# A fixed order of 1254 steps replaced by another fixed order

## The chip, the cores and the metric

The kernel runs on one core of one Trainium2 chip. The metric is the device time of one execution in microseconds (us). The engines are PE (TensorE; PEld is its weight load), DVE (VectorE), ACT (ScalarE), POOL (GpSimd) and SP (SyncE, which here only starts transfers).

## What is computed

Linear attention over 8 batches of 8 heads feeds a gated MLP (gMLP). All data are fp32.

```python
q_s = softmax(q, axis=-1);  k_s = softmax(k, axis=2)      # q, k, v: (8, 8, 576, 64)
kv  = einsum('bhsd,bhde->bhde', k_s, v)                   # k_s^T v for each head
x   = einsum('bhsd,bhde->bhse', q_s, kv)                  # heads side by side: (8, 576, 512)
h   = gelu_tanh(x @ w_in);  u, v = h[..., :512], h[..., 512:]
v_n = (v - mean(v)) / sqrt(var(v) + 1e-6) * g_ln
v_s = einsum('ts,bsd->btd', w_sg, v_n) + b_sg[None, :, None]
out = x + (u * v_s) @ w_out
```

(The first einsum sums over the 576 positions s.)

## The kernel before, in words

Every large product is made of three PE products of high and low fp32r parts (high by high, high by low, low by high), so each operand is first split: ACT writes the rounded high part, DVE or POOL subtracts to get the low part. In the names of tiles `_h` is the high part and `_l` the low one, and `vnh`, `vnl`, `gh`, `ulow` are such parts too.

The work is cut into 1254 steps, each a small function called with a batch number and indices, and the text `PLAN` (from line 39) lists all of them in one fixed order. The loop at line 920 reads it and calls one function after the other. Each of DVE, ACT, POOL and SP runs its instructions strictly in the order in which the steps issue them (class `InOrder`), and PE keeps program order too. So the order in `PLAN` decides what stands behind what on each engine. An engine whose next instruction waits makes everything behind it wait. A letter at the end of a step names the engine where there is a choice (V is DVE, G is POOL, A is ACT).

The steps that the text speaks of:

- Weights arrive as 64-bit words in eight pieces f for `w_in` (`load_w_in f`) and four for `w_out`. ACT scales a piece (`wi_a f`), DVE repairs the bits in three instructions (`wi_b`, `wi_c`, `wi_d`), ACT writes the high part (`wi_h`), and `wi_l` the low part. The tile in work is `ot_i`. Pieces 4 to 7 are needed by `hv_mm`, 0 to 3 by `hu_part` and `hu_mm`.
- For each batch b and half of the heads h: `k_sub` and `k_exp` make the exponent of k (tile `kk`), `kv_mm` multiplies it by v, `kv_inv` and `kv_scale` (DVE, tile `kvt`) divide. `q_sub`, `q_exp`, `q_sum` (tile `qd`), `q_swapd` (ACT, tile `qe`), `q_inv` and `q_mul` make the softmax of q (tile `qq`), and `q_turn` transposes it into `qt`. `x_mm` (batch 1) or `xm_mm` (batches 2 to 7) multiply kv by q.
- `hv_mm b i` and `hv_gelu` make v (through two PSUM banks, `ps1`, that are used in turn, also by `kv_mm`). `hv_sq`, `hv_stat`, `hv_pow` (POOL), `hv_norm`, `hv_high` and `hv_low` normalise it and split it into `vnh` and `vnl`.
- `sg_mm`, `hu_mm` and `out_mm` use three double banks (`ps2`) in turn. A bank comes free when `gate`, `hu_gelu` or `out_add` has read it.
- `gate b d` (DVE) is u times v_s, `gate_high` and `gate_low` split it, `out_mm b e` multiplies it by `w_out`, `out_base` adds the two parts of x, `out_add` adds the product, and `out_store` writes the result.

ACT must load a table (ACT_TABLE_LOAD) whenever it goes from exponentials to gelu or back. The compiler puts it right before the first instruction that needs it.

Of the kernel before, what the change touches and what calls it, by code (L numbers as in the profile page):

```python
# [63 lines left out]
hv_pow 0 2, k_mb 2 1, k_mc 2 1, hv_high 0 2, hv_stat 0 4 A, hv_pow 0 4, tail_high 1, k_mb 2 0, k_mc 2 0, load_w_sg 4, ws_h 4, tail_high 0, hv_low 0 2
k_fold 2 1, wo_h 2, hv_mm 1 2, hv_gelu 1 2, k_rota 2 1, ws_l 4 V, k_maxa 2 1, hv_mm 1 1, k_rotb 2 1, ws_l 2 G, tail_again 0, hv_sq 1 3, tail_low 0
ws_l 3 G, sg_mm 0 0, sg_mm 0 2, k_fold 2 0, hv_sq 1 0, k_maxb 2 1, q_max 2 1, q_swapm 2 1, hv_stat 1 0 A, k_rota 2 0, k_sub 2 1 G, q_max 2 0
tail_low 1, k_maxa 2 0, hv_gelu 1 1 A, load_v 2 1, q_top 2 1, q_sub 2 1 G, gate 0 0, k_rotb 2 0, hv_sq 1 1, q_swapm 2 0, k_exp 2 1, q_exp 2 1
sg_mm 0 1, gate_high 0 0, gate 0 2, hv_stat 1 1 A, wo_l 2 G, sg_mm 0 3, wo_l 1 V, hu_mm 1 0, gate_low 0 0 G, gate 0 1, hv_norm 1 0, hv_pow 1 0
k_maxb 2 0, k_sub 2 0 V, q_top 2 0, k_exp 2 0, gate 0 3, gate_high 0 3, gate_high 0 1, q_sub 2 0 V, gate_low 0 1 V, hv_stat 1 3 A, wo_h 3, wo_l 3 G
gate_high 0 2, hv_stat 1 2, load_v 2 0, gate_low 0 2 G, q_exp 2 0, q_sum 2 0, q_swapd 2 0, q_sum 2 1, out_base 0 2 V, wo_l 0 V, gate_low 0 3 G  # L70
kv_mm 2 1, hv_high 1 0, hv_low 1 0, out_base 0 3 V, hv_pow 1 2, kv_mm 2 0, load_k 3 1, k_ma 3 1, out_mm 0 3, q_inv 2 0, q_mul 2 0 1 G, hv_pow 1 1
kv_inv 2 0, load_k 3 0, out_mm 0 1, out_add 0 3, q_swapd 2 1, q_inv 2 1, hu_gelu 1 0, out_mm 0 0, q_mul 2 1 1 V, q_turn 2 1, q_mul 2 0 0 V, q_turn 2 0
out_mm 0 2, out_base 0 1 V, out_base 0 0 G, out_add 0 1, q_mul 2 1 0 G, hv_pow 1 3, hu_mm 1 3, kv_inv 2 1, out_add 0 0, kv_scale 2 1, hu_gelu 1 3
hv_norm 1 2, load_q 3 0, q_turn 2 3, out_add 0 2, out_store 0 2, kv_scale 2 0, hv_norm 1 3, q_max 3 0, hv_norm 1 1, hv_high 1 3, hu_mm 1 2
hv_high 1 1, out_base 1 2 G, q_turn 2 2, hv_low 1 1, k_mb 3 1, k_mc 3 1, hv_low 1 3, hv_high 1 2, k_fold 3 1, k_ma 3 0, hv_low 1 2, hu_gelu 1 2
q_swapm 3 0, q_top 3 0, xm_mm 2, tail_again 1, xm_high 2 0, sg_mm 1 0, xm_high 2 1, xt_high 2, load_q 3 1, xt_low 2, xm_low 2 0, hu_mm 1 1, q_max 3 1
q_swapm 3 1, xm_low 2 1, q_sub 3 0 V, gate 1 0, q_top 3 1, out_store 0 3, k_mb 3 0, k_mc 3 0, out_store 0 1, sg_mm 1 2, k_rota 3 1, k_maxa 3 1
q_sub 3 1 V, load_v 3 0, k_fold 3 0, hu_gelu 1 1, q_exp 3 0, k_rota 3 0, k_maxa 3 0, k_rotb 3 0, q_exp 3 1, hv_mm 2 1, hv_mm 2 3, k_maxb 3 0
q_sum 3 1, gate_high 1 0, sg_mm 1 1, q_sum 3 0, hv_gelu 2 1 A, k_rotb 3 1, k_sub 3 0 G, out_base 1 3 V, hv_gelu 2 3, k_maxb 3 1, k_sub 3 1 G, gate 1 2
gate_low 1 0 V, sg_mm 1 3, hv_sq 2 1, gate 1 1, load_v 3 1, out_base 1 1 G, q_swapd 3 1, q_inv 3 1, q_mul 3 1 0 V, q_turn 3 2, hv_stat 2 1 A  # L80
k_exp 3 0, kv_mm 3 0, kv_inv 3 0, k_exp 3 1, kv_scale 3 0, q_swapd 3 0, gate_high 1 2, gate 1 3, q_inv 3 0, gate_high 1 1, q_mul 3 0 1 V
out_store 0 0, kv_mm 3 1, kv_inv 3 1, kv_scale 3 1, out_base 1 0 G, gate_low 1 1 G, gate_low 1 2 G, hv_pow 2 1, q_mul 3 1 1 V, q_turn 3 3
gate_high 1 3, q_mul 3 0 0 G, hv_mm 2 0, hv_gelu 2 0 A, q_turn 3 1, q_turn 3 0, hv_sq 2 0, hv_stat 2 3, gate_low 1 3 G, out_mm 1 2, load_q 4 1
# [892 lines left out]
```

## Time before, and how to read the profile

| | |
|---|---|
| median of 3 runs | 500.97 us (500.81 to 501.94) |
| profiled execution | 500.59 us, of which the span from first to last instruction is 498.5 us |
| PE busy | 481.5 us, 97% of the span |
| DVE busy | 359.7 us, 72% |
| ACT busy | 282.6 us, 57%, with 32 table loads (41.1 us) |
| POOL busy | 159.8 us, 32% |
| granted PE clock | full level (2.4 GHz) in all 40 slices |

The rows further down come from one profiled execution. A timeline row has its start in us, its duration in us, the engine, the line of the kernel (a helper issues nearly everything, so the line is always the same), the operation, out<-in by tile, and in brackets how long the engine sat idle before it and what ended that. A row with x40 merges 40 instructions. Busy PE includes matmuls that are slowed, and their ends are modelled, so distances between starts are the better measure there.

### The profile page before, as it was taken

To read this page: it belongs to the slowest core of one execution; us is meant where nothing else is said; L and a number is where in the kernel's file an instruction comes from. 1 tells how busy PE (TensorE), PEld (TensorE's weight loads), DVE (VectorE), ACT (ScalarE), POOL (GpSimd) and SP (SyncE) were. 2 spreads that over 40 slices of the span, in tenths; PEclk is the share of its full clock that TensorE was granted. 3 is DMA by queue.
4 is the path that set the end of the run, shared out by engine and by line. 5 is a ranking of instruction groups with operands and counts; after the bars stand their busy time and mean duration, and the time that the engine had idled before them with its cause. 6 is when DMAs were issued, how large, how long until landed. Compare 5 with 4: busy or idle time off the path is not lost.

```text
span 498.5 us, 9491 instructions
## 1 busy us (share of the span) xinstructions
PE 481.5 (97%) x3847; PEld 444.6 (89%) x3847; DVE 359.7 (72%) x618; ACT 282.6 (57%) x605; POOL 159.8 (32%) x126
## 2 busy tenths in 40 slices
...
GB/s 308 384 380 169 171 121 2 94 63 236 4 1 262 106 26 1 7 219 0 168 2 101 174 47 16 104 1 130 217 2 0 46 51 1 1 0 49 49 1 95
DMA packets 16302, 47.51 MB, mean 95 GB/s; under 512 B 1922, under 2 KB 3332, under 8 KB 16260
## 3 DMA queue, kind: packets, MB, share of 16 engines
...
## 4 chain that ended last, share of the span: by engine, by line
PE 52%; DVE 18%; ACT 11%; POOL 2%; issue 2%; ACTq 0%; POOLq 0%; DVEq 0%
PE ps L253 52%; DVE qq L164 3%; DVE qd L164 3%; DVE km L164 2%; POOL kk L164 2%; DVE o L164 2%; ACT L164 2%; DVE qm L164 1%; ACT v L164 1%; DVE qt L164 1%; DVE kf L164 1%; ACT kk L164 1%; ACT ka L164 1%; ACT gh L164 1%; ACT qq L164 1%
## 5 line engine op out<-in xcount | busy, mean ns | idle before, releaser
L164 POOL TENSOR_TENSOR rs<-ve,half 128x1 f32<-128x1 f32 x36 | 29.3, 821 | 131.3 <-DVE ve L164 118.1
L253 PE MATMUL ps<-ulow,wo_h 128*128 128x288 f32 x256 | 55.6, 296 | 0.8 <-POOL ulow L164 0.8
L253 PE MATMUL ps<-gh,wo_h 128*128 128x288 f32 x256 | 55.9, 297 | 0.0
L253 PE MATMUL ps<-ws_h,vnl 128*128 128x288 f32 x256 | 55.0, 296 | 0.5 <-DVE vnl L164 0.5
L253 PE MATMUL ps<-ws_h,vnh 128*128 128x288 f32 x256 | 55.3, 297 | 0.2 <-DVE u L164 0.2
L253 PE MATMUL ps<-gh,wo_l 128*128 128x288 f32 x256 | 55.4, 295 | 0.0
L253 PE MATMUL ps<-ws_l,vnh 128*128 128x288 f32 x256 | 54.9, 296 | 0.0
L164 DVE TENSOR_TENSOR u<-ps,u 128x576 f32<-128x576 f32 x32 | 23.5, 746 | 42.5 <-PE ps L253 37.6
L164 ACT ACTIVATE u<-ps 128x576 f32<-128x576 f32 (+2 forms) x36 | 21.2, 595 | 42.7 <-PE ps L253 42.5
L164 ACT ACT_TABLE_LOAD x32 | 41.1, 1283 | 2.9 <-PE ps L253 1.2
L164 ACT CAST gh<-u 128x576 fp32r<-128x576 f32 x32 | 20.8, 668 | 38.4 <-DVE u L164 38.3
L253 PEld LDWEIGHTS ps<-ulow,wo_h 128*128 128x128 f32 x256 | 41.3, 188 | 1.1 <-POOL ulow L164 1.1
L253 PEld LDWEIGHTS ps<-ws_h,vnh 128*128 128x128 f32 x256 | 41.3, 188 | 1.0 <-DVE u L164 0.4
L253 PE MATMUL ps<-x_h,wi_h 128*128 128x288 f32 (+2 forms) x256 | 40.6, 298 | 1.4 <-DVE o L164 0.8
L253 PEld LDWEIGHTS ps<-gh,wo_h 128*128 128x128 f32 x256 | 41.4, 188 | 0.6
L253 PEld LDWEIGHTS ps<-ws_h,vnl 128*128 128x128 f32 x256 | 41.1, 188 | 0.7 <-DVE vnl L164 0.7
L253 PEld LDWEIGHTS ps<-gh,wo_l 128*128 128x128 f32 x256 | 41.4, 188 | 0.0
L253 PEld LDWEIGHTS ps<-ws_l,vnh 128*128 128x128 f32 x256 | 41.0, 188 | 0.0
L164 DVE TENSOR_TENSOR o<-ps,o 128x576 f32<-128x576 f32 (+1 forms) x33 | 23.9, 732 | 23.2 <-PE ps L253 22.5
L253 PE MATMUL ps<-x_h,wi_l 128*128 128x288 f32 (+2 forms) x256 | 39.9, 296 | 0.0
L253 PE MATMUL ps<-x_l,wi_h 128*128 128x288 f32 (+2 forms) x256 | 39.8, 295 | 0.0
L253 PE MATMUL ps<-wi_h,x_h 128*128 128x512 f32 x144 | 39.5, 396 | 0.3 <-ACT wi_h L164 0.2
(128 smaller groups left out, 1089.8 us busy)
## 6 DMA issues: line engine op xcount, KB each, us to landing
...
```

The source lines that it names most:

```text
L164: ins = op(*args, **kw)
L253: tc.keep_in_program_order(nc.tensor.matmul(*args, **kw))
```

## The change

The text `PLAN` is replaced. The 1254 steps are the same, but 67 of them change between V and G, and nearly all stand elsewhere. By kind, the steps that DVE gives to POOL on balance are 5 `gate_low`, 4 `q_mul`, 2 `q_sub` and 2 `wo_l`. POOL gives to DVE 2 `k_sub`, 3 `out_base` and 1 `ws_l`. DVE has 7 instructions fewer, POOL 7 more. ACT has 34 table loads for 32. Nothing else is edited. A few lines of the text, cut:

```diff
 PLAN = """
...
-k_top 1 0, q_swapm 1 0, k_top 1 1, wi_a 6, hu_part 0 3 0, hu_gpart 0 3 0, wi_l 7 V, q_exp 1 1, kb_mm 1 0, wi_b 6, wi_c 5, kb_mm 1 1, wi_c 6, q_top 1 0
-load_w_out 2, q_swapd 1 0, hv_mm 0 0, kv_scale 1 0, q_inv 1 0, q_mul 1 0 0 V, load_w_out 1, b_l G, q_mul 1 0 1 G, hv_gelu 0 0 A, ws_h 1, q_turn 1 0
-q_mul 5 0 0 V, k_maxa 5 1, hv_gelu 4 3, hv_stat 4 0 A, sg_mm 3 2, hu_gelu 3 2, hv_gelu 4 1 A, k_rotb 5 1, k_exp 5 0, k_maxb 5 1, q_turn 5 0
-out_store 2 1, k_sub 5 1 G, k_exp 5 1, gate_high 3 1, hv_stat 4 3, q_swapd 5 1, q_inv 5 1, gate 3 3, load_v 5 0, hv_mm 4 2, hv_gelu 4 2
-out_base 3 1 G, kv_mm 5 0, gate 3 2, gate_high 3 2, q_turn 5 1, gate_low 3 1 V, q_mul 5 1 0 G, gate_low 3 2 V, hv_sq 4 1, hv_pow 4 3, gate_high 3 3
...
+wi_a 6, wi_a 5, wi_d 4, hu_gpart 0 0 0, k_top 1 0, wi_h 4, load_w_sg 2, k_top 1 1, q_max 1 0, wi_h 7, hu_part 0 1 0, hu_gpart 0 1 0, load_w_out 3
+q_sum 1 0, wi_l 4 G, wi_h 5, wi_l 5 G, kv_mm 1 0, kv_inv 1 0, b_l G, k_exp 1 1, q_swapd 1 0, q_sum 1 1, kv_scale 1 0, hu_gpart 0 2 1, load_w_sg 3
+q_swapd 1 1, hv_mm 0 0, hv_gelu 0 0 A, q_inv 1 0, wo_a 3, q_mul 1 0 0 V, q_turn 1 0, q_inv 1 1, wo_a 0, q_mul 1 1 0 V, load_g, hu_gpart 0 3 1
+q_turn 5 1, k_exp 5 1, hv_norm 4 0, gate_low 3 1 G, gate 3 2, hv_norm 4 2, gate_high 3 2, hu_mm 3 3, q_turn 5 3, hv_high 4 3, gate_low 3 2 V
+k_exp 5 0, kv_mm 5 1, kv_inv 5 1, hu_gelu 3 3, kv_mm 5 0, gate 3 3, gate_high 3 3, gate_low 3 3 G, load_q 6 1, kv_inv 5 0, load_q 6 0, load_v 6 1
...
```

Three places show what the new text does to the order on an engine. In each pair the first fence is the kernel before.

DVE, batch 1, where pieces 4 to 7 of `w_in` are repaired (`ot_i_6` is piece 6, `ot_i_5` piece 5, `kt1` and `qm1` are maxima of k and q, `kk1_0` is k of half 0):

```order
L164 TENSOR_REDUCE qm1_0_445<-qq1_0_373 128x36
L164 TENSOR_REDUCE kt1_0_449<-ps1_0_80 128x2
L164 TENSOR_REDUCE kt1_1_456<-ps1_1_81 128x2
L164 TENSOR_TENSOR wi_l_62<-ot_i_7_317,wi_h_61 128x4x128
L164 TENSOR_SCALAR ot_i_6_458<-ot_i_6_458 128x512
L164 SCALAR_TENSOR_TENSOR ot_i_5_405<-raw_i_wo_h_91,ot_i_5_405 128x512
L164 SCALAR_TENSOR_TENSOR ot_i_6_458<-raw_i_wo_l_92,ot_i_6_458 128x512
L164 TENSOR_TENSOR qm1_0_445<-qm1_0_445,qs1_0_451 128x36
L164 SCALAR_TENSOR_TENSOR ot_i_6_458<-raw_i_wo_l_92,ot_i_6_458 128x512
```

The same place on DVE now:

```order
L163 TENSOR_REDUCE kt1_0_442<-ps1_0_80 128x2
L163 TENSOR_REDUCE kt1_1_447<-ps1_1_81 128x2
L163 TENSOR_REDUCE qm1_0_449<-qq1_0_354 128x36
L163 TENSOR_SCALAR ot_i_6_436<-ot_i_6_436 128x512
L163 TENSOR_TENSOR wi_l_62<-ot_i_7_331,wi_h_61 128x4x128
L163 SCALAR_TENSOR_TENSOR ot_i_6_436<-raw_i_wo_l_92,ot_i_6_436 128x512
L163 TENSOR_SCALAR ot_i_5_438<-ot_i_5_438 128x512
L163 SCALAR_TENSOR_TENSOR ot_i_6_436<-raw_i_wo_l_92,ot_i_6_436 128x512
L163 TENSOR_TENSOR qm1_0_449<-qm1_0_449,qs1_0_468 128x36
```

Piece 6 is now begun before `wi_l` of piece 7 and ends before piece 5. On ACT its `wi_a 6` has moved ahead of `wi_h 4`, `wi_h 7`, some gelus and the `q_swapm 1 0` copies, all of which stood before it. `load_w_in 6` has moved one place up on SP's queue, past `load_q 1 0`.

ACT, batches 0 and 1, at the first table load for gelu behind the exponentials of batch 1 (`qe1_0` and `qe1_1` are `q_swapd 1 0` and `1 1`, `u0_2` is gelu of u, `v0_0` is `hv_gelu 0 0`, `ws_h` and `ot_o` are weights):

```order
L164 ACTIVATE kk1_1_368<-kk1_1_368 128x1280
L164 COPY qe1_0_571<-qd1_0_563 32x36 x4
L164 ACT_TABLE_LOAD
L164 ACTIVATE v0_0_598,sm0_0_599<-ps1_0_80 128x512
L164 CAST ws_h_63<-ghws_1_492 128x576
L164 COPY qe1_1_604<-qd1_1_568 32x36 x4
L164 ACTIVATE u0_1_439<-ps2_2_79 128x320
L164 ACTIVATE u0_2_447<-ps2_0_77 128x320
```

The same place on ACT now:

```order
L163 ACTIVATE kk1_1_340<-kk1_1_340 128x1280
L163 COPY qe1_0_575<-qd1_0_544 32x36 x4
L163 ACT_TABLE_LOAD
L163 ACTIVATE u0_2_414<-ps2_2_79 128x320
L163 COPY qe1_1_587<-qd1_1_580 32x36 x4
L163 ACTIVATE v0_0_604,sm0_0_605<-ps1_0_80 128x512
L163 ACTIVATE ot_o_3_609<-raw_o_vnl_365 128x512
L163 ACTIVATE ot_o_0_616<-raw_o_vnh_372 128x512
```

The table load now stands before a gelu of `u0_2`, whose product `hu_part 0 2 1` is made before `kv_mm 1 0`, and `q_swapd 1 1` stands before `hv_gelu 0 0`.

DVE, outputs of batch 0 (`o0_e<-ps2...,o0_e` is `out_add 0 e`, `o0_e<-x_h0,x_l0` is `out_base 0 e`, `kr2` and `kvt2` are `kv_inv` and `kv_scale` of batch 2, `v1` is `hv_norm`, `qt2` is `q_turn`):

```order
L164 TENSOR_TENSOR o0_1_1345<-x_h0_308,x_l0_310 128x576
L164 TENSOR_TENSOR o0_1_1345<-ps2_0_77,o0_1_1345 128x576
L164 TENSOR_SCALAR kr2_1_1377<-ps1_0_80 128x2
L164 RECIPROCAL kr2_1_1377<-kr2_1_1377 128x2
L164 TENSOR_TENSOR o0_0_1347<-ps2_1_78,o0_0_1347 128x576
L164 TENSOR_TENSOR kvt2_1_1381<-ps1_0_80,kr2_1_1377 128x128
L164 SCALAR_TENSOR_TENSOR v1_2_895<-v1_2_895,mv1_2_1150,g_bc_67 128x512
L164 STREAM_TRANSPOSE qt2_1_1388<-qq2_1_725 128x576
L164 TENSOR_TENSOR o0_2_1169<-ps2_2_79,o0_2_1169 128x576
```

The same place on DVE now:

```order
L163 TENSOR_TENSOR o0_3_1215<-ps2_2_79,o0_3_1215 128x576
L163 TENSOR_TENSOR o0_0_1326<-x_h0_303,x_l0_308 128x576
L163 SCALAR_TENSOR_TENSOR v1_2_995<-v1_2_995,mv1_2_1138,g_bc_67 128x512
L163 TENSOR_SCALAR kr2_1_1332<-ps1_1_81 128x2
L163 RECIPROCAL kr2_1_1332<-kr2_1_1332 128x2
L163 TENSOR_TENSOR kvt2_1_1335<-ps1_1_81,kr2_1_1332 128x128
L163 TENSOR_TENSOR o0_1_1246<-ps2_1_78,o0_1_1246 128x576
L163 TENSOR_TENSOR o0_2_1253<-ps2_0_77,o0_2_1253 128x576
```

The bank `ps2_0_77`, which `hu_mm 1 3` takes next on PE in both kernels, is read by `out_add 0 1` before and by `out_add 0 2` now, directly behind `out_add 0 1`.

On PE, `kv_mm 5 0` and `5 1` stood right behind `hv_mm 4 2`. Now `sg_mm 3 3` and `hu_mm 3 3` stand between `hv_mm 4 1` and them.

## Rows read from the trace of the kernel before

**Rows 1.** The page, first line: span of the profiled execution.

```profile
span 498.5 us, 9491 instructions
```

**Rows 2.** Stretches: us, busy us (instructions) by engine, PE clock, DMA share, GB/s.

```profile
4.00:34.00 30.00, 26.35 (x252) 21.91 (x253) 29.55 (x62) 26.10 (x51) 12.41 (x10) 1.00 1.02 386
34.00:52.00 18.00, 16.04 (x160) 13.29 (x161) 14.59 (x24) 16.55 (x33) 11.94 (x9) 1.00 0.52 180
52.00:98.00 46.00, 45.66 (x350) 40.10 (x342) 43.56 (x79) 39.03 (x101) 25.83 (x19) 1.00 0.29 96
98.00:155.00 57.00, 54.75 (x469) 49.38 (x468) 53.03 (x88) 32.63 (x71) 25.09 (x18) 1.00 0.27 89
...
270.00:495.00 225.00, 225.00 (x1736) 214.12 (x1734) 136.10 (x230) 98.73 (x203) 45.56 (x37) 1.00 0.16 58
```

**Rows 3.** Waits of PE, 98 to 155 us: total us, times, longest us.

```profile
PE ps L253 <- POOL ulow L164: 0.8, 1, 0.8
PE ps L253 <- DVE o L164: 0.8, 1, 0.8
PE ps L253 <- DVE vnl L164: 0.5, 1, 0.5
```

**Rows 4.** Timeline of DVE near 34 us: start, us, instruction, [idle before <-releaser].

```profile
33.65 0.70 DVE L164 TENSOR_TENSOR wi_l<-ot_i,wi_h 128x512 fp32r<-128x512 f32 x1
35.62 0.43 DVE L164 TENSOR_SCALAR ot_i<-ot_i 128x512 uint32<-128x512 uint32 x1 [1.27 <-ACT ot_i L164]
```

**Rows 5.** Timeline of ACT near 35 us.

```profile
34.92 0.67 ACT L164 ACTIVATE ot_i<-raw_i_wo_l 128x512 f32<-128x512 f32 x1
```

**Rows 6.** Timeline of ACT, 45 to 49 us.

```profile
45.53 1.28 ACT L164 ACT_TABLE_LOAD   x1 [1.17 <-PE ps L253]
46.83 0.60 ACT L164 ACTIVATE v<-ps 128x512 f32<-128x512 f32 x1
...
48.23 0.91 ACT L164 COPY qe<-qd 32x36 f32<-32x36 f32 x4
```

**Rows 7.** Timeline of DVE near 49 us.

```profile
49.17 0.20 DVE L164 SCALAR_TENSOR_TENSOR qd<-qd,qe 128x36 f32<-128x36 f32 x1 [1.93 <-ACT qe L164]
```

**Rows 8.** Timeline of PE, 40 to 57 us.

```profile
40.74 1.39 PE L253 MATMUL ps<-vv,kk 128*64 128x65 f32 x40 [0.71 <-ACT kk L164]
...
49.65 0.70 PE L253 MATMUL ps<-qt,kvt 64*64 64x288 f32 x2
51.32 1.20 PE L253 MATMUL ps<-qt,kvt 64*64 64x288 f32 x14 [0.97 <-DVE qt L164]
52.44 1.19 PE L253 MATMUL ps<-wi_h,x_h 128*128 128x512 f32 x4
...
55.42 1.20 PE L253 MATMUL ps<-qt,kvt 64*64 64x288 f32 x16
56.55 0.53 PE L253 MATMUL ps<-x_h,minus 128*128 128x288 f32 x2
```

**Rows 9.** Timeline of PE near 268 us.

```profile
268.29 0.92 PE L253 MATMUL ps<-vv,kk 128*64 128x65 f32 x24 [1.29 <-ACT v L164]
```

**Rows 10.** DVE groups, 98 to 155 us: count | busy us, mean ns | idle before.

```profile
L164 DVE TENSOR_TENSOR qq<-qq,qd 128x576 f32<-128x576 f32 x5 | 7.8, 1562 | 0.1
...
L164 DVE TENSOR_TENSOR ulow<-u,gh 128x576 fp32r<-128x576 f32 x1 | 3.1, 3079 | 0.0
```

**Rows 11.** Tile qd on DVE, whole span: duration ns min/median/max.

```profile
L164 DVE TENSOR_TENSOR qq<-qq,qd x17: 695/758/2033, 13.3 to 381.8; 128x576 f32<-128x576 f32 x16, 128x512 f32<-128x512 f32 x1
L164 DVE SCALAR_TENSOR_TENSOR qd<-qd,qe x14: 155/198/2947, 44.8 to 362.3; 128x36 f32<-128x36 f32 x14
```

**Rows 12.** POOL groups, whole span: count | busy us, mean ns | idle before.

```profile
L164 POOL TENSOR_TENSOR kk<-kk,km 128x1280 f32<-128x1280 f32 x9 | 27.0, 3004 | 38.1 <-issue 15.9 <-DVE km L164 12.4 <-PE ps L253 9.7
L164 POOL TENSOR_TENSOR ulow<-u,gh 128x576 fp32r<-128x576 f32 x16 | 24.8, 1550 | 30.7 <-ACT gh L164 16.2 <-DVE ulow L164 14.3
...
L164 POOL TENSOR_TENSOR qq<-qq,qd 128x576 f32<-128x576 f32 (+2 forms) x15 | 19.5, 1298 | 34.3 <-DVE qd L164 27.8 <-ACT u L164 2.8 <-ACT kb L164 2.4
```

More of the change, by code (lines that the diff above doesn't have):

```diff
@@ L64 @@
[L64 to L83, printed above, removed]
@@ L100 @@
-hv_gelu 4 0 A, q_swapm 5 1, q_top 5 1, hu_mm 3 3, k_maxa 5 0, out_add 2 3, out_store 2 3, hv_low 3 3, hv_low 3 2, k_mb 5 1, q_sub 5 1 G, q_exp 5 1
-hv_pow 3 0, hv_high 3 0, out_store 2 0, hv_low 3 0, hv_sq 4 0, hv_mm 4 1, hu_gelu 3 3, hu_mm 3 1, hu_gelu 3 1, q_swapm 5 0, q_top 5 0, k_mc 5 1
-k_fold 5 1, q_sub 5 0 V, q_sum 5 1, sg_mm 3 0, sg_mm 3 1, out_base 3 3 G, k_rotb 5 0, q_exp 5 0, q_sum 5 0, k_maxb 5 0, hv_mm 4 3, k_sub 5 0 G
-out_base 3 0 V, load_v 5 1, q_swapd 5 0, q_inv 5 0, gate 3 0, gate 3 1, hu_mm 3 2, gate_high 3 0, gate_low 3 0 G, sg_mm 3 3, k_rota 5 1, q_mul 5 0 1 G
@@ new lines @@
+k_maxa 3 1, k_maxb 3 0, sg_mm 1 0, q_swapm 3 0, q_top 3 0, hu_mm 1 1, hu_gelu 1 1, k_sub 3 0 V, gate 1 0, k_rotb 3 1, k_maxb 3 1, out_store 0 0
+hv_mm 2 3, q_sub 3 0 G, q_exp 3 0, sg_mm 1 1, sg_mm 1 3, q_sum 3 0, gate 1 1, k_exp 3 0, q_swapd 3 0, gate_high 1 1, gate_high 1 0, out_base 1 0 V
+k_sub 3 1 G, k_exp 3 1, sg_mm 1 2, q_inv 3 0, hv_mm 2 1, q_top 3 1, q_sub 3 1 V, gate_low 1 0 G, q_exp 3 1, q_sum 3 1, hv_gelu 2 3, gate 1 2, gate 1 3
+q_mul 3 0 0 G, q_mul 3 0 1 G, q_swapd 3 1, q_inv 3 1, hv_gelu 2 1 A, gate_high 1 2, kv_mm 3 1, kv_inv 3 1, hv_sq 2 1, gate_low 1 1 G, kv_scale 3 1
@@ new lines @@
+q_swapm 4 1, q_inv 4 0, k_mb 4 0, k_mc 4 0, q_top 4 1, hu_mm 2 2, q_sub 4 1 G, q_mul 4 0 0 G, q_exp 4 1, hv_pow 2 4, tail_high 2, q_sum 4 1
+k_fold 4 0, hv_low 2 2, tail_again 2, hu_gelu 2 2, q_turn 4 0, hv_norm 3 2, hv_mm 3 3, hu_mm 2 1, tail_high 3, tail_low 3, hv_sq 3 1, hu_mm 2 0
+k_rota 4 0, out_base 2 3 G, hu_gelu 2 1, q_swapd 4 1, hv_gelu 3 0 A, tail_low 2, sg_mm 2 1, hu_gelu 2 0, sg_mm 2 0, q_mul 4 0 1 G, sg_mm 2 3
+q_inv 4 1, k_maxa 4 0, hv_pow 3 2, k_rotb 4 0, k_maxb 4 0, q_turn 4 1, gate 2 1, gate_high 2 1, gate 2 0, hv_gelu 3 3 A, gate_high 2 0, load_q 5 0
@@ new lines @@
+sg_mm 3 1, q_inv 5 0, hv_gelu 4 3, out_add 2 3, k_fold 5 0, q_sub 5 1 V, q_exp 5 1, q_sum 5 1, hu_mm 3 1, hu_gelu 3 1, gate 3 1, hv_stat 4 3
+hv_norm 4 3, q_swapd 5 1, k_rota 5 0, k_maxa 5 0, q_mul 5 0 0 G, sg_mm 3 0, sg_mm 3 2, gate 3 0, hv_gelu 4 2, hv_sq 4 0, q_mul 5 0 1 G, k_rotb 5 0
+hv_pow 4 3, q_inv 5 1, q_mul 5 1 0 V, k_sub 5 1 V, hv_stat 4 2, hv_pow 4 2, hv_stat 4 0 A, hv_pow 4 0, hu_mm 3 2, hu_gelu 3 2, hv_mm 4 1
+hv_gelu 4 1 A, q_turn 5 2, gate_high 3 1, q_mul 5 1 1 V, gate_high 3 0, out_store 2 0, k_maxb 5 0, sg_mm 3 3, q_turn 5 0, k_sub 5 0 G, gate_low 3 0 G
```

167 lines of the change are left out of this document (89 added, 78 removed).

## The prediction

> **What bounds the kernel now.** I read the table of stretches first. From 270 us to the end PE is busy for all of 225 us [rows 2], so nothing that another engine does there can shorten the time, it can only add a wait. What an order can win lies earlier. From 4 to 34 us DVE is busy 29.55 of 30 us and the transfers run at 1.02 of their engines [rows 2]: there DVE has no slack, and PE follows it. From 34 to 52 us no engine is full: PE 16.04, DVE 14.59, ACT 16.55 of 18 us [rows 2]. Three engines that all have gaps in one stretch are waiting for each other, so this is the first place to look at. From 52 to 98 us PE is full (45.66 of 46). From 98 to 155 us DVE is nearly full again, 53.03 of 57, and PE has waits that add up to 2.1 us: for an `out_add`, for a `gate_low` and for an `hv_low` [rows 2, 3].
>
> Next I read the timelines of the stretch from 34 to 52 us, engine by engine. DVE stops for 1.27 us before `wi_b 6` [rows 4], because ACT comes to `wi_a 6` only at 34.92 us [rows 5]. ACT was not waiting for that piece, it stood behind other ACT work. DVE stops a second time, 1.93 us before `q_inv 1 1` [rows 7]. The reader should follow that one back: it waits for the copies of `q_swapd 1 1`, which start at 48.23 us, behind a table load that itself waited 1.17 us for PE before it began at 45.53 [rows 6]. The load is tied to the gelu behind it, and that gelu needs the end of `hv_mm 0 0`. On PE the two stops appear as 0.71 us ahead of `kv_mm 1 0` and as a long `x_mm 1 0`: 2.79 us from its start at 49.65 to the next step at 52.44, where `x_mm 1 1` takes 1.13 (55.42 to 56.55) [rows 8].
>
> **The change part by part.** The work is the same, so the sum is one of waits.
>
> Term A, the stretch from 34 to 52 us. `wi_a 6` is moved ahead on ACT, and `wi_b 6` follows `q_max 1 0`, with `wi_l 7` behind it. The 1.27 us on DVE go, since ACT is free of what held it. Behind them stand `wi_d 5`, `k_sub 1 0` and everything later on DVE, so all of this comes 1.27 us earlier, and with it the exponent that `kv_mm 1 0` waits for. The table load now precedes a gelu of `hu_part 0 2 1`, a product that PE makes several steps earlier, so its 1.17 us of waiting go too, and `q_swapd 1 1` stands one gelu and one weight copy closer: 45.53 less 1.17 is 44.36, plus 1.28 for the load and some 0.6 for a gelu is 46.2, where it was 48.23 [rows 6]. That is 2.0 us earlier, more than the 1.93 that DVE waited. So DVE wins up to 1.27 + 1.93 = 3.2 us. PE cannot win more than it lost: 0.71 + (2.79 - 1.13) = 2.37 us. I take all of it, **2.4 us**; the other end is 0.7, if something else holds `x_mm 1 0`. One thing moves the other way: `load_q 1 0` comes behind `load_w_in 6` on SP's queue, 0.52 MB at 386 GB/s [rows 2], 1.4 us later. It feeds `q_max 1 0`, which the new order puts behind both `k_top`; that covers some of it, and without cover the 1.4 us would eat the first of the two gains.
>
> Term B, 98 to 155 us. DVE comes here with a lead of up to 3.2 us over before, PE with 2.4. Against it: `hu_mm 1 3` takes the bank that `out_add 0 2` frees, one DVE instruction later than before. For its cost I take another DVE operation on 128x576, 0.76 us (the median in [rows 11]). The lead of DVE less PE is 0.8, so this spot comes out about level. What is better for sure is that the waits for `out_add` and for `hv_low` (0.8 + 0.5 [rows 3]) came in a chain in which DVE was late, and it is less late now. I take these **1.3 us** as won and leave the 0.8 for `gate_low` as it is; the ends are 0 and 2.1. ACT has two table loads fewer up to the start of `hv_mm 2 0`, 2 x 1.28 = 2.6 us [rows 6], which lies in its idle time (32.63 busy of 57 [rows 2]) and is counted at nothing. It would be worth 1.28 each where PE waits for ACT.
>
> Term C, the wait at 268 us: `kv_mm 5 1` needs the bank of `hv_mm 4 2`, and `hv_gelu 4 2` comes late on ACT, 1.29 us [rows 9]. In the new order `sg_mm 3 3` and `hu_mm 3 3` stand in between on PE, so that gelu is long done. **1.3 us** won; the other end is nothing, if the exponents are late instead.
>
> Term D, new waits behind 155 us. Four table loads more stand there on ACT, and where one stands ahead of an `hv_gelu` the same trap is set. `hv_mm 4 0`, `4 2` and `4 3` now follow each other on PE. The third needs the bank of the first, whose gelu stands behind `q_exp 5 0`, `k_rota 5 1` and a table load. There is one `hv_mm` between, 2.98 us (52.44 to 55.42 [rows 8]), for 1.28 + 0.60 us [rows 6] of load and gelu. That leaves 1.1 us if ACT is on time, so it is fragile. I take one wait like that at 268 us, **1.3 us lost**; the ends are 0 and 2.6 (two of them).
>
> The rest comes out at nothing. Before 34 us the order of DVE's work changes but not its amount; the cover is DVE itself (29.55 of 30 [rows 2]), with ends of 0.45 won and one late transfer, 1.4, lost. On balance five `gate_low` and four `q_mul` go from DVE to POOL and two `k_sub` come back: 5 x 1.55 + 4 x 1.30 - 2 x 3.00 = 7 us more on POOL, by its mean durations [rows 12]. The other moves (`q_sub`, `wo_l` against `out_base`, `ws_l`) I leave at zero, as they go both ways. POOL was busy 25.09 of 57 us in the tight stretch [rows 2], so the work itself fits; what it does to DVE is the second rival.
>
> The sum: -2.4 - 1.3 - 1.3 + 1.3 = -3.7 us. The profiled execution took 500.59 us (its span of 498.5 [rows 1] and 2.1 around it), so this gives 496.9. That execution lies 0.4 under the median of the runs shown, hence **497.2 us**.
>
> **DVE and POOL take turns.** The row that shows it best: `q_inv`, 128x36, has a median of 0.198 us and a longest of 2.947 [rows 11], about the length of a POOL `k_sub`, 3.00 [rows 12]. The five `q_mul` on DVE from 98 to 155 us took 1.56 on average against a median of 0.76 [rows 10, 11], and one `gate_low` 3.08. That is 5 x 0.80 + 2.3 = 6.3 us of DVE's 53. The Trainium skill says this as a rule (SBUF — State Buffer, section "SBUF: two separate sides"): a VectorE operation with two SBUF inputs and a GpSimd operation that reads SBUF share a port pair, whichever starts first holds it for its whole instruction, and the other blocks fully. The trace agrees: the longest `q_inv` is as long as a POOL instruction, not a little longer than itself. The page speaks against moving work to POOL beside a full DVE. By the row I leave the turns in the tight stretch at the 6.3 us that they cost now. By the rule taken strictly, each of the 7 us more on POOL could hold DVE as long, 7 us in all, of which only what falls between 52 and 155 us reaches PE; the second rival gives that its time.
>
> **The rivals.** First, the lead is given back: the turns from 52 to 155 us cost 3.2 us more than before, DVE arrives at 155 us as late as it did, and C and D cancel. The time is then that of before, 500 to 501. For it speaks that the new order puts `q_mul 3 0 0`, `q_mul 3 0 1`, `q_mul 3 1 1` and `gate_low 1 0` all on POOL in that stretch; against it, that four of the DVE operations that were held are gone from DVE.
>
> Second, it becomes slower: the place is the same stretch, and the mechanism that DVE is held by POOL twice as long as before, 6.3 us more. Less the lead of 3.2 that is 3.1 us of new PE waits; with C and D cancelling, 500.97 + 3.1 = 504. It decides against the kernel from the point where the turns cost 3.2 + 1.0 us more than before.
>
> Third, everything goes well: B is won whole (2.1) and D is nothing. -2.4 - 2.1 - 1.3 = -5.8, so 495.2.
>
> **How the numbers follow.** About 1.0 us (0.2%) is what a measurement of this kernel can tell from no change. The forecast, 495.9 to 499, gets 0.55; the third rival 0.18; the first 0.13; slower 0.14. The forecast and the third rival make faster, and a part of the first too: 0.75 faster, 0.12 same, 0.13 slower. The likeliest case alone reaches from 495.2 to 499.3. For 8 in 10 I take 494.0 to 501.4: under the third rival by DVE's 0.45 and the other end of C and D together, and up through the first.
>
> **What would show it.** A is right if DVE has no idle time ahead of `wi_b 6` and `q_inv 1 1`, the table load ahead of `q_swapd 1 1` starts without waiting, and `x_mm 1 0` takes about 1.1 us. B is right if PE's waits from 98 to 155 us sum to under 1 us. C is right if `kv_mm 5` has no wait, and D shows as a PE wait for an ACT `v` between 200 and 300 us. The prediction is wrong if DVE's `q_mul` and `gate_low` in the tight stretch grow on average above 2 us, or if a transfer ends a wait of DVE before 52 us.

## The result, and the profile after

The changed kernel takes 495.52 us (median of 4, 494.03 to 495.75), the kernel before 500.89 (4 runs, 500.53 to 501.94): a ratio of 0.9883, with a 95% interval from 0.9858 to 0.9908. That is 5.4 us faster and 1.7 us below the predicted 497.2: inside the range that was given 8 chances in 10 (494.0 to 501.4), but under the lower end of the forecast itself (495.9) and close to the third rival's 495.2.

The profiled execution took 495.75 us. Its span, and the stretches that answer to [rows 2] (columns as there):

```profile
span 494.0 us, 9497 instructions
4.00:34.00 30.00, 25.13 (x234) 21.52 (x235) 27.45 (x59) 24.82 (x48) 11.63 (x11) 0.94 0.98 358
34.00:52.00 18.00, 18.00 (x183) 15.67 (x182) 17.38 (x28) 17.66 (x38) 14.53 (x10) 1.00 0.80 277
98.00:155.00 57.00, 56.66 (x466) 52.46 (x468) 49.32 (x91) 29.39 (x70) 22.24 (x17) 1.00 0.33 110
```

The gaps from 34 to 52 us are closed on three engines at once: PE is full (16.04 before), DVE has 17.38 for 14.59. From 98 to 155 us PE gained 1.9 us of busy time while DVE's fell from 53.03 to 49.32. The first row got worse: PE 25.13 for 26.35, DVE 27.45 for 29.55, and the granted clock fell to 0.94.

PE's waits in the changed kernel, from 4 to 34 us and, the last line, from 98 to 155, which answers to [rows 3]; the list of its waits from 155 us to the end is empty:

```profile
PE ps L252 <- DMA eye<-identity: 4.4, 1, 4.4
PE ps L252 <- DVE qq L163: 2.3, 1, 2.3
PE ps L252 <- ACT x_lk L163: 1.6, 1, 1.6
...
PE ps L252 <- DVE o L163: 0.3, 1, 0.3
```

ACT at the table load of term A, DVE at `wi_b 6` and at `q_inv 1 1`, and PE at `x_mm 1 0`, which answer to [rows 4, 6, 7, 8]:

```profile
45.42 1.28 ACT L163 ACT_TABLE_LOAD   x1
46.71 0.44 ACT L163 ACTIVATE u<-ps 128x320 f32<-128x320 f32 x1
47.16 0.91 ACT L163 COPY qe<-qd 32x36 f32<-32x36 f32 x4
...
35.57 0.42 DVE L163 TENSOR_SCALAR ot_i<-ot_i 128x512 uint32<-128x512 uint32 x1
48.10 0.30 DVE L163 SCALAR_TENSOR_TENSOR qd<-qd,qe 128x36 f32<-128x36 f32 x1
...
50.48 1.20 PE L252 MATMUL ps<-qt,kvt 64*64 64x288 f32 x16
51.61 1.19 PE L252 MATMUL ps<-wi_h,x_h 128*128 128x512 f32 x4
```

None of these has a bracket behind it: no wait. `x_mm 1 0` takes 1.13 us where it took 2.79.

**Where the time went.** Start times of single steps mislead here, because the order differs. I therefore took, for each product on PE, the time from its start to the next start, less the shortest such time of its kind, and summed this loss over the same products, sorted by the stretch in which the kernel before starts them. In us, for all kernels but e11 and e12, which have products that the others lack; the times are medians, and the kernel before took 500.7 to 500.9 beside them:

```
kernel                  to 28  28-52  52-98  98-155  155-270  270-end   time
before                   8.9    4.1    1.7    4.1      3.6      2.1    500.9
changed                 10.8    1.1    1.7    1.4      2.0      2.4    495.5
e1_bias_later            8.7    2.0    1.8    1.4      2.0      2.3    495.9
e2_q_earlier            10.7    1.1    1.7    1.3      2.0      2.4    495.5
e3_both_loads           11.0    2.1    1.8    1.4      1.9      2.4    495.8
e4_letters              10.7    2.6    3.5    4.9      4.5      2.5    505.3
e10_stretch              9.7    1.1    2.3    5.7      2.0      2.4    498.6
e6_late_load             9.0    2.2    2.1    4.2      3.6      2.3    499.1
e7_term_a                9.0    2.2    2.0    4.1      3.6      2.0    499.1
e8_term_c                9.0    4.0    1.7    4.2      5.1      1.9    502.3
e9_engines_only         10.5    4.1    9.1    9.0      5.6      9.2    520.8
```

From before to changed, taken before rounding: +1.9, -3.0, +0.1, -2.8, -1.6, +0.3, together -5.1 us. The two profiled executions differ by 4.8; the first product starts 0.2 us later in the changed one (4.39 for 4.15), which the table does not count.

### The profile page after: what moved, and what is told of

It is laid out like the page before. It is cut to its first block, busy times and chain, and to the rows that moved or that the text cites. A ratio compares the mean times of both kernels' runs of the same rounds, so it can differ in the third digit from the quotient of the medians.

```text
span 494.0 us, 9497 instructions
## 1 busy us (share of the span) xinstructions
PE 480.7 (97%) x3847; PEld 445.6 (90%) x3847; DVE 348.5 (71%) x611; ACT 285.6 (58%) x607; POOL 168.8 (34%) x133
## 4 chain that ended last, share of the span: by engine, by line
PE 80%; DVE 9%; DMA 3%; ACT 3%; POOL 2%; issue 2%; SPq 0%; POOLq 0%
PE ps L252 80%; DMA raw_i_vnh<-w_in 1%; DVE v L163 1%; DMA vv<-v 1%; POOL qq L163 1%; DVE ot_i L163 1%; DVE ot_o L163 1%; POOL wi_l L163 1%; DVE km L163 1%; DVE o L163 1%; DMA eye<-identity 1%; DVE vnl L163 1%; ACT L163 1%; ACT kk L163 0%; DVE qt L163 0%
## 5 line engine op out<-in xcount | busy, mean ns | idle before, releaser
L163 POOL TENSOR_TENSOR ulow<-u,gh 128x576 fp32r<-128x576 f32 x21 | 33.4, 1593 | 90.0 <-ACT gh L163 48.5
L163 POOL TENSOR_TENSOR rs<-ve,half 128x1 f32<-128x1 f32 x36 | 26.2, 734 | 96.3 <-DVE ve L163 96.3
L163 POOL TENSOR_TENSOR qq<-qq,qm 128x1152 f32<-128x1152 f32 (+2 forms) x10 | 20.9, 2092 | 67.5 <-DVE qm L163 26.8
L163 ACT ACTIVATE vnh<-v,rs 128x512 fp32r<-128x512 f32 x32 | 22.9, 723 | 33.0 <-DVE v L163 18.4
```

The source lines that it names most:

```text
L163: ins = op(*args, **kw)
```

## The experiments

**Term A on the kernel before.** First the late table load alone (e6), then with `wi_a 6` ahead (e7, whose first two rows are the part that e6 does not have; `wi_a 6` leaves the row below them):

```diff
-wi_d 4, hu_part 0 1 0, q_top 1 1, kt_mm 1 1, hu_part 0 2 0, q_sub 1 1 G, b_h, hu_gpart 0 1 0, wi_h 4, kt_mm 1 0, wi_b 5, q_max 1 0, hu_gpart 0 2 0
+wi_d 4, hu_part 0 1 0, q_top 1 1, kt_mm 1 1, hu_part 0 2 0, q_sub 1 1 G, b_h, hu_gpart 0 1 0, wi_a 6, wi_h 4, kt_mm 1 0, wi_b 5, q_max 1 0, hu_gpart 0 2 0
...
-load_w_out 2, q_swapd 1 0, hv_mm 0 0, kv_scale 1 0, q_inv 1 0, q_mul 1 0 0 V, load_w_out 1, b_l G, q_mul 1 0 1 G, hv_gelu 0 0 A, ws_h 1, q_turn 1 0
+load_w_out 2, q_swapd 1 0, hu_gpart 0 2 1, q_swapd 1 1, hv_mm 0 0, kv_scale 1 0, q_inv 1 0, q_mul 1 0 0 V, load_w_out 1, b_l G, q_mul 1 0 1 G, hv_gelu 0 0 A, ws_h 1, q_turn 1 0
```

> The kernel before with one part of the change: hu_gpart 0 2 1 and q_swapd 1 1 ahead of hv_mm 0 0, so that the table load in front of the gelu stands ahead of a gelu whose product is long there. Theory (second half of term A): the load starts without its 1.17 us of waiting, DVE's 1.93 us ahead of q_inv 1 1 go, x_mm 1 0 takes about 1.1 us where it took 2.8, and hv_mm 0 1 starts 1.6 us earlier, at 50.8. If DVE's lead is also what took the waits out of the stretch from 98 to 155 us, these shrink as well and the time is near 497.5; if that was the choice of engines, PE's waits there stay at about 2 us and the time is 499.1. Rival: the stop is another one in disguise, x_mm 1 0 stays at 2 us or more, and the time at 500.7.

> The kernel before with both parts of term A: the former edit, and wi_a 6 moved ahead of wi_h 4 on ACT. Theory: DVE's 1.27 us ahead of wi_b 6 go too, kv_mm 1 0 starts 0.7 us earlier, hv_mm 0 1 2.4 us earlier (50.0), and the time is 498.3 if the stretch from 98 to 155 us gains nothing by that lead, 496.5 to 497 if it does. Rival: wi_a 6 only moves ACT's lateness to what stood ahead of it (wi_h 4, q_swapm 1 0), and this kernel is no faster than the one with the late load alone.

Measured: e6 499.11 us, ratio 0.9972 (0.9962 to 0.9981); e7 499.12, ratio 0.9965 (0.9952 to 0.9979). In e6's timeline of ACT the load has lost its wait, and in that of PE `x_mm 1 0` is short:

```profile
44.70 1.28 ACT L164 ACT_TABLE_LOAD   x1
...
49.79 1.20 PE L253 MATMUL ps<-qt,kvt 64*64 64x288 f32 x16
50.92 1.21 PE L253 MATMUL ps<-wi_h,x_h 128*128 128x512 f32 x4
```

The second half of term A is right, by itself and at its size: 1.55 us of time, against 1.66 that PE lost there. The first half is worth nothing by itself. In e7, DVE comes to `wi_b 6` without its 1.27 us of idle time, but stops 1.1 us for an exponent of q instead, and PE's `kv_mm 1 0` waits as before: it waits for an exponent of k that stands behind other work on ACT, which is busy for 6.89 of the 7 us from 34 to 41:

```profile
40.88 1.33 PE L253 MATMUL ps<-vv,kk 128*64 128x65 f32 x38 [0.65 <-ACT kk L164]
```

And both show what the early lead does later: PE's waits from 98 to 155 us are the three of [rows 3] to the tenth, 0.8, 0.8 and 0.5. DVE and PE come there earlier together, by 1.1 us in e6 and 1.3 in e7, and their distance stays. So the lead of term A is not what won term B.

**The engines, apart from the order.** e4 keeps the new order and puts all 67 steps back on their old engine. e9 does the reverse: old order, new engines. e10 puts back only the 16 steps from 90 to 155 us, of which three rows stand here:

```diff
-load_v 3 0, gate_low 0 1 G, gate_low 0 2 G, kv_mm 2 1, load_k 3 0, q_exp 2 0, wo_l 2 G, load_v 3 1, wo_l 0 G, gate 0 3, gate_high 0 3, q_exp 2 1
+load_v 3 0, gate_low 0 1 V, gate_low 0 2 G, kv_mm 2 1, load_k 3 0, q_exp 2 0, wo_l 2 G, load_v 3 1, wo_l 0 V, gate 0 3, gate_high 0 3, q_exp 2 1
...
-out_mm 0 1, q_inv 2 0, q_mul 2 0 1 G, out_add 0 3, load_k 3 1, hv_pow 1 2, out_base 0 0 V, q_mul 2 1 1 G, hv_high 1 0, hv_norm 1 2, hv_high 1 2
+out_mm 0 1, q_inv 2 0, q_mul 2 0 1 G, out_add 0 3, load_k 3 1, hv_pow 1 2, out_base 0 0 G, q_mul 2 1 1 V, hv_high 1 0, hv_norm 1 2, hv_high 1 2
...
-hv_low 1 0, hu_mm 1 2, hu_gelu 1 2, out_store 0 1, k_ma 3 0, q_turn 2 1, q_mul 2 0 0 G, q_turn 2 0, out_add 0 0, kv_scale 2 0, xm_mm 2, hv_low 1 2
+hv_low 1 0, hu_mm 1 2, hu_gelu 1 2, out_store 0 1, k_ma 3 0, q_turn 2 1, q_mul 2 0 0 V, q_turn 2 0, out_add 0 0, kv_scale 2 0, xm_mm 2, hv_low 1 2
```

> The changed order with all 67 steps that changed between DVE and POOL put back on the engine that they had before; the order is that of the changed kernel. If the choice of engine is what took PE's waits out of the stretch from 98 to 155 us, they come back: 2 to 3 us more there, about 498. If DVE's earlier arrival and the order are what did it, PE's waits there stay under 1 us, and the time is within 1 us of 495.5. Either way the turns of DVE and POOL show in the mean durations of q_mul and gate_low.

> The order of the kernel before, with all 67 steps that changed between DVE and POOL on the engine that the changed kernel gives them. The reverse (the changed order with the old engines) was 4.5 us slower than before. If the new choice of engines is better by itself, DVE is held less by POOL and this is 1 to 3 us faster than before, 498 to 499.5. If order and engines only work as a pair, since an order is made for the moments at which POOL works, this is slower than before as well, 502 to 506.

> The changed order, with only those 16 steps put back on their old engine (DVE or POOL) that ran between 90 and 155 us. Theory: which engine does these steps decides how long POOL holds DVE there (by the trace 8.4 us before, 3.7 in the changed kernel), and that is what took PE's waits out of this stretch. Then DVE's single operations grow again by 2 us or more in sum, PE's waits from 98 to 155 us come back to 2 us or more, and the time is 497.5 to 499. Rival: the order of the products on PE took the waits out, and the engines matter elsewhere (the first test put all 67 back and lost 9.7 us). Then PE's waits there stay under 1 us and the time is near 495.5.

Measured: e4 505.25 us, ratio 1.0081 (1.0065 to 1.0096); e9 520.76, ratio 1.0409 (1.0387 to 1.0431); e10 498.59, ratio 0.9956 (0.9944 to 0.9969). The order alone is 4.5 us slower than before, the engines alone 20 us, the two together 5.4 us faster: there is no share of the gain that belongs to the one or the other. Not all of the 20 us is waiting: in e9's profiled execution PE's granted clock falls to its lower level three times behind a longer pause, once behind the 3.7 us shown below:

```profile
162.00:169.00 7.00, 6.52 (x41) 3.70 (x42) 1.90 (x4) 1.29 (x4) 1.34 (x2) 0.51 0.94 311
```

The three falls cover 13.7 us; as an estimate, PE loses half of that, 6.8 of the 22.8 us by which this execution is longer than the profiled one before. e10 says where the engines count: those 16 steps, of which eight go to DVE and eight to POOL, carry 3.1 us, and PE's loss from 98 to 155 us goes from 1.4 to 5.7. Its waits there:

```profile
PE ps L252 <- DVE kvt L163: 1.4, 1, 1.4
PE ps L252 <- ACT v L163: 1.2, 2, 0.8
PE ps L252 <- DVE o L163: 0.9, 2, 0.5
```

What an engine's choice does can be seen on DVE. In the kernel before, POOL is first with a `k_sub`, then DVE comes to a `gate_low` (timelines of POOL and DVE near 137 us):

```profile
136.44 2.95 POOL L164 TENSOR_TENSOR kk<-kk,km 128x1280 f32<-128x1280 f32 x1 [1.54 <-DVE km L164]
136.93 3.08 DVE L164 TENSOR_TENSOR ulow<-u,gh 128x576 fp32r<-128x576 f32 x1
```

POOL's ends at 139.39, DVE's at 140.01: what DVE's took is the rest of POOL's and then about its own 0.7. The changed kernel has the same on another pair:

```profile
125.75 3.26 POOL L163 TENSOR_TENSOR qq<-qq,qm 128x1152 f32<-128x1152 f32 x1 [18.03 <-DVE qm L163]
127.60 1.44 DVE L163 TENSOR_TENSOR kf<-kf,kb 128x8 f32<-128x8 f32 x1
```

An operation on 128x8 takes 0.17 us elsewhere (at 135.72 in the kernel before); here it ends 0.03 us after POOL's. The rule of the Trainium skill that the prediction weighed (SBUF — State Buffer, section "SBUF: two separate sides") says just this, and the two pairs agree with it. What it does not say is how much of that is bound to happen. I summed what each DVE instruction took over its usual time (the held time): from 98 to 155 us 8.5 us before, 3.7 in the changed kernel, 6.9 in e4, 6.9 in e10. The groups that were long in [rows 10] are now, on DVE in that stretch (tiles ulow and qq of the changed kernel: duration min/median/max, ns):

```profile
L163 DVE TENSOR_TENSOR ulow<-u,gh x2: 716/716/717, 142.9 to 145.5; 128x576 fp32r<-128x576 f32 x2
L163 DVE TENSOR_TENSOR qq<-qq,qd x2: 747/752/757, 100.9 to 143.5; 128x576 f32<-128x576 f32 x2
```

and in e10:

```profile
L163 DVE TENSOR_TENSOR qq<-qq,qd x4: 708/1020/1321, 103.6 to 146.5; 128x576 f32<-128x576 f32 x4
```

The held time is not all of it. In e10 DVE also stands still for 1.33 us, because `q_mul 2 1 0` is now on POOL and `q_turn 2 2` needs it:

```profile
101.78 0.78 DVE L163 STREAM_TRANSPOSE qt<-qq 128x576 f32<-128x576 f32 x1 [1.33 <-POOL qq L163]
```

How much of e10's 3.1 us is held time and how much is such results that come later was not separated. Nor is it excluded that DVE is held less partly because POOL has less to do there: it is busy for 22.24 us of the stretch in the changed kernel, for 25.09 before, 25.10 in e10 and 27.74 in e4. Against this as the only reason stands the stretch from 155 to 270 us, where POOL is busy for 41.70 us instead of 35.79 and the held time is about the same, 8.8 and 8.9 us (an operation's median over the kernels taken as its usual time). And e9 has only 4.3 us of held time from 98 to 155 us, and yet a loss of 9.0; its longest wait, from 155 to 270 us, is an order that does not fit its engines, 3.7 us for a `ve` on DVE:

```profile
PE ps L253 <- DVE ve L164: 3.7, 1, 3.7
```

**Term C on the kernel before** (e8): `hu_mm 3 3` between `hv_mm 4 2` and `kv_mm 5 0`, with its gelu and gate.

```diff
-out_store 2 1, k_sub 5 1 G, k_exp 5 1, gate_high 3 1, hv_stat 4 3, q_swapd 5 1, q_inv 5 1, gate 3 3, load_v 5 0, hv_mm 4 2, hv_gelu 4 2
+out_store 2 1, k_sub 5 1 G, k_exp 5 1, gate_high 3 1, hv_stat 4 3, q_swapd 5 1, q_inv 5 1, load_v 5 0, hv_mm 4 2, hu_mm 3 3, hv_gelu 4 2, hu_gelu 3 3
```

> The kernel before with hu_mm 3 3 (and its gelu and gate) moved between hv_mm 4 2 and kv_mm 5 0, as in the changed order. Theory (term C): the wait of 1.3 us ahead of kv_mm 5 1 goes and nothing takes its place, 499.3. Rival: DVE and ACT are late there anyway, and the wait moves to out_mm 3 2 or to what follows where hu_mm 3 3 stood: 500.7 or more.

Measured: 502.26 us, ratio 1.0036 (1.0023 to 1.0049), slower by 1.6 (the profiled execution, 501.82, by 1.2). The rival was right. The wait of [rows 9] is gone. Where `hu_mm 3 3` stood, at 232.6 us, PE now comes to `sg_mm 3 0` without that product in between, and inside it waits twice, 2.0 us in all (waits of PE from 155 to 270 us):

```profile
PE ps L253 <- DVE vnl L164: 1.1, 1, 1.1
PE ps L253 <- ACT vnh L164: 0.9, 1, 0.9
```

**The start.** Two things had moved: `load_b A` to the front of ACT's queue, and `load_q 0 0 1` behind two loads of k. Three kernels take them back in the changed order: e1 the bias (first pair of rows; it goes behind `wi_a 7`), e2 the load of q (second pair), e3 both.

```diff
-load_eye A, warm 0, load_q 0 1 1, warm 2, qf_max 0 1 1, qf_sub 0 1 1 V, load_q 0 1 0, qf_max 0 1 0, warm 4, qf_sub 0 1 0 G, load_q 0 0 0, load_b A
+load_eye A, warm 0, load_q 0 1 1, warm 2, qf_max 0 1 1, qf_sub 0 1 1 V, load_q 0 1 0, qf_max 0 1 0, warm 4, qf_sub 0 1 0 G, load_q 0 0 0
...
-qf_max 0 0 0, qf_exp 0 1 1, qf_sum 0 1 1, load_k 0 0 1, load_k 0 0 0, qf_sub 0 0 0 G, warm 7, b_h, kr_max 0 0 1, load_k 0 1 0, load_q 0 0 1
+qf_max 0 0 0, qf_exp 0 1 1, qf_sum 0 1 1, load_k 0 0 1, load_q 0 0 1, load_k 0 0 0, qf_sub 0 0 0 G, warm 7, b_h, kr_max 0 0 1, load_k 0 1 0
```

> The changed order, with the two small transfers of the bias and their two copies put back where the kernel before has them. First theory: the two transfers take two of the eight landing semaphores that the first transfers use in turn, so the transfers of q and k behind them start late, and with them DVE, PE and PE's clock up to 28 us. Then no transfer of SP's first seven waits before it is issued, DVE's wait of 1.0 us for q_flat is gone, the granted clock stays above 0.9 from 14 to 20 us, hu_part 0 0 1 starts near 26.3 us (28.2 in the changed kernel) and the time is near 493.6. Rival: the new order of DVE's and PE's own steps at the start (the first k transpose ahead of the q transposes, qf_mul 0 0 0 on DVE) loses the time. Then PE still waits about 2 us for DVE's qq, hu_part 0 0 1 stays near 28, and the time at 495.5.

> The changed order, with the transfer load_q 0 0 1 alone put back to the fifth place of SP's queue; the bias transfers stay early. If it is the lateness of this one transfer that costs the start, DVE's wait for q_flat goes, hu_part 0 0 1 starts near 26.5 us and the time is near 494. If the two k transfers, which now wait for a landing semaphore in its place, matter as much, it stays between 27.5 and 28.5 us, and the time between 495 and 496. If the order of the engines' own steps is the cause, PE's wait for qq stays at 2 us or more, and nothing changes (495.5).

> Both edits together: bias later and load_q 0 0 1 in fifth place. If the transfers are the whole cause of the 2.1 us that the start lost, this is the kernel before's order of transfers, hu_part 0 0 1 starts at 26 to 26.4 us and the time is 493.4 to 493.8. If the engines' own order at the start is the cause, it stays at 495.5, with hu_part 0 0 1 near 28. If half and half, 494.5.

Measured: e1 495.91 us (494.55 to 496.23), ratio 0.989 (0.9872 to 0.9907); e2 495.48 (493.76 to 495.71), ratio 0.9871 (0.985 to 0.9892); e3 495.80 (494.79 to 498.15), ratio 0.9899 (0.9877 to 0.9921). The transfers came earlier, and that alone is not enough. In all three DVE's second wait for `q_flat` (1.00 us at 10.53 in the changed kernel) is gone, and yet no median is clearly below the changed kernel's 495.52. e1 won the start back in its profiled execution (`hu_part 0 0 1` at 26.04) but lost 0.9 us from 28 to 52 us, where the two copies of the bias now stand on ACT, and its other four executions had a granted clock of 0.996 to 0.997. e3 has the transfers of the kernel before and the worst start of all. The timelines of PE near 10 us show what is left, first the changed kernel, then e2:

```profile
4.39 4.39 PE L252 MATMUL ps<-eye 128*128 128x128 f32 x20 [4.39 <-DMA eye<-identity]
10.40 1.31 PE L252 MATMUL ps<-eye,x_lk 128*128 128x128 f32 x10 [1.62 <-ACT x_lk L163]
14.53 0.65 PE L252 MATMUL ps<-eye,qq 128*128 128x128 f32 x4 [2.27 <-DVE qq L163]
15.12 2.39 PE L252 MATMUL ps<-vv,kk 128*64 128x65 f32 x40
```

```profile
10.51 2.40 PE L252 MATMUL ps<-eye,x_lk 128*128 128x128 f32 x10 [1.37 <-ACT x_lk L163]
```

The same ten products take 1.31 or 2.40 us, `kv_mm 0 0` 1.39 or 2.39. PE runs there at its lower level, 1.2 GHz. The clock in windows of 2 us says the same (the last number but two), of the changed kernel

```profile
14.00:16.00 2.00, 1.47 (x22) 1.30 (x24) 1.93 (x6) 2.00 (x5) 1.48 (x2) 0.80 1.03 414
16.00:18.00 2.00, 2.00 (x30) 1.88 (x28) 0.99 (x4) 2.00 (x4) 1.38 (x2) 0.50 1.03 387
```

and of e3:

```profile
14.00:16.00 2.00, 2.00 (x22) 1.67 (x24) 1.93 (x5) 2.00 (x6) 1.57 (x2) 0.50 1.03 410
```

In the old order seven dummy steps (`warm`, two products each) stand ahead of the first transposes, in the new one five. At what moment PE comes to the full rate (109 ns for a product of 128 columns, 213 before) differs between executions, and the count of dummies does not settle it: in the kernel before it comes in the fifth of the seven, in e6 and e7, which have the same order, only behind the seventh; in the changed kernel in the last of the five, in e1 and e10 in the pause behind them, in e2 only at 13.95 us, after fifteen slow transposes. Then PE pauses, in the changed kernel for 1.6 and 2.3 us, where the two pauses of the kernel before were 0.7 and 0.9, and behind such pauses the rate falls again in the changed kernel, e3 and e4, but not in e10, whose pauses are 1.4 and 2.1. So one profile proves little here. Taken together, none of the five profiles of the old order (before, e6 to e9) has a real product at the lower rate in the first 20 us, and four of the six of the new order without further dummies have some. e11 and e12 add dummies in two places, e11 five and nine, e12 five and five together with the load of q of e2 (the rows are e11's first place):

```diff
+    def fill(n):
+        ps = ps2[(count[id(ps2)] + 1) % 3]
+        for i in range(n):
+            mm(ps[:, i % 2, 0:P], eye, eye, start=True, stop=True)
...
-kr_exp 0 1 0, warm 8, ktr_mm 0 0, qf_sum 0 1 0, kr_rest 0 0, load_v 0 0, qf_sum 0 0 0, qf_inv 0 0 0, qf_inv 0 1 0, qf_sub 0 0 1 G, qf_exp 0 0 1
+kr_exp 0 1 0, warm 8, fill 5, ktr_mm 0 0, qf_sum 0 1 0, kr_rest 0 0, load_v 0 0, qf_sum 0 0 0, qf_inv 0 0 0, qf_inv 0 1 0, qf_sub 0 0 1 G, qf_exp 0 0 1
```

> The changed order with dummy products added on PE at the start: five behind warm 8 and nine behind qtr_mm 0 1 1, where PE otherwise stops for 1.6 and 2.5 us. Theory: the start lost its 2.1 us since the new order has five dummies ahead of the first real product where the old one has seven, so that PE comes to its full rate (109 ns for a product of 128 columns, 213 at the half level) only at the end of the last, and falls back in its pauses. With the dummies no product from 10 to 20 us takes 213 ns, the granted clock stays at 1.0 in every execution, kv_mm 0 0 takes 1.4 us, hu_part 0 0 1 starts near 27 us and the time is near 494. Rival: DVE, which waits 1.0 us for a transfer, sets the start: 495.5, with the dummies only filling pauses.

> The changed order with load_q 0 0 1 in fifth place of SP's queue and five dummy products each behind warm 8 and behind qtr_mm 0 1 1. The transfer alone gave executions of two kinds, two near 493.8 and three near 495.6; in a profile of the second kind the products from 10.5 to 14 us took 213 ns each. If PE's rate was what divided them, all executions are now near 493.8 or a little below, hu_part 0 0 1 starts at 26 to 26.5 us, and this is the fastest kernel, 493.3 to 493.9. Rival: the two kinds come from the transfers' landing, and the dummies change nothing: 495.5, or both kinds again.

Measured: e11 494.70 us (494.28 to 495.05), ratio 0.9877 (0.9862 to 0.9893); e12 493.92 (493.74 to 494.13), ratio 0.9862 (0.9849 to 0.9876). `hu_part 0 0 1` starts at 27.18 and 26.76 us (26.09 before, 28.20 changed), and from there on both lose what the changed kernel loses. In e12's timeline of PE no real product is at the lower level. Its full rate came at 7.4 us, ahead of all added dummies; what these did is to fill the second pause, 0.1 us for 2.3:

```profile
10.62 1.31 PE L252 MATMUL ps<-eye,x_lk 128*128 128x128 f32 x10 [1.25 <-ACT x_lk L163]
...
14.29 1.39 PE L252 MATMUL ps<-vv,kk 128*64 128x65 f32 x40
```

e12 has the lowest median of all. Of the changed kernel's four executions only the 494.03 lies among e12's, but the two intervals overlap, so that the 1.6 us between the medians are likely rather than settled. In e11 DVE still has the late transfer, and it is 0.8 us slower than e12: clock and transfer each seem to have a part, about 0.8 us each, and in the medians the transfer's shows only where dummies fill the pauses. The 0.7 us by which e12's `hu_part 0 0 1` is still later than before stay unexplained.

## Why the prediction was right

**Term A** was put at 2.4 us, and 3.0 were won. Its second half, the late load, is shown at its size (e6). Its first half, 0.7 for `wi_a 6`, failed as a step: what the prediction put as "so all of this comes 1.27 us earlier, and with it the exponent that `kv_mm 1 0` waits for" did not follow, because that exponent stands at the end of ACT's own full queue (e7). The changed kernel has no wait there either, but by which of its other moves was not isolated; this is about 1.1 of the 3.0 us.

**Term B** was put at 1.3 us and became 2.8 from 98 to 155 us, above its own upper end of 2.1; the 0.8 for `gate_low` that was left as it is went too. The step that failed is "it is less late now": in e6 and e7 DVE gets a lead, but PE gets the same one, and every wait stays. And "By the row I leave the turns in the tight stretch at the 6.3 us that they cost now" left out the term that moved most. The two kinds of operation behind those 6.3 us are not held at all any more where DVE does them (0.72 and 0.75 us). A row of held operations shows what they cost in one order; another order meets POOL at other moments. The first two rivals took the turns as a given too, and made them longer. POOL's added work did come, 168.8 us busy for 159.8, but not in the tight stretch, where it has 2.9 us less.

**Term C** was put at 1.3 us, and 1.6 were won from 155 to 270 us, 1.4 of them at `kv_mm 5 0` and `5 1`. The wait went, but the reason given is only half of it: the single move costs 1.6 us (e8). It pays in an order that does not wait where the product stood.

**Term D**, 1.3 us lost, did not happen. The rows are the load, the gelu of `hv_mm 4 0` and its sum on ACT, and the start of `hv_mm 4 3` on PE:

```profile
227.91 1.28 ACT L163 ACT_TABLE_LOAD   x1 [0.17 <-DVE vnl L163]
229.21 0.60 ACT L163 ACTIVATE v<-ps 128x512 f32<-128x512 f32 x1
229.70 0.19 ACT L163 ACTIVATION_READ_ACCUMULATOR v<-ps 128x1 f32 x1
...
231.78 1.09 PE L252 MATMUL ps<-wi_h,x_h 128*128 128x512 f32 x4
```

The gelu has ended at 229.89, so the slack that the prediction worked out as 1.1 us was 1.9: the load ran beside `hv_mm 4 0`, which PE did until 228.99, and not behind it. That "fragile" wait had then been counted whole.

**The start** was put at nothing, with "one late transfer, 1.4, lost" as its end. It lost 1.9 us in the profiled execution, more than that end. The late transfer is there, DVE waits 1.0 us for it, and by the letter this is one of the two signs that the prediction named for being wrong (a transfer ends a wait of DVE before 52 us; the kernel before has such a wait too, at the very first load). But e1 to e3 and e11 put the transfer at no more than about half. PE's clock behind its dummies and pauses, which the prediction did not look at, is the likely rest.

B was put 1.5 us too high in time, D 1.0 (1.3, less the 0.3 more that is lost behind 270 us), A and C 0.6 and 0.3, and the start 1.9 too low. So the sum came out 1.4 us off while its terms are 5.3 off: that it is this close is luck, since the start's loss hid over half of what the others won more. The number is near the third rival's 495.2, but not by that rival's road.
